# An attention kernel with a fused gated expert layer: another hand-written order for the first fourteen steps

## The chip, the cores and the metric

The kernel runs on one core of one Trainium2 chip. The metric is the device time of one execution in microseconds (us); smaller is better. The core has five engines with a queue each: PE (matrix products), DVE (vector work), ACT (functions of one input, scaled copies), POOL (vector work, slower, no access to the accumulators), and SP (which here only issues transfers). Each engine takes its instructions in the order of its own queue and waits on semaphores for the others.

## The reference

Two parts, all in float32, with inputs q, k, v of 4 batches, 8 heads, 768 positions, 64 features, and expert weights of 512 x 2048 and 2048 x 512:

```python
k_sum = k.reshape(B, H, nb, 32, D).max(axis=3)      # 24 block maxima of the keys
v_sum = v.reshape(B, H, nb, 32, D).mean(axis=3)     # 24 block means of the values
a = softmax(concat[mask_l(scale * q @ k.T), scale * q @ k_sum.T + log(32)])   # window of +-15
x = (a @ concat[v, v_sum]).reshape(3072, 512)
h = x @ w_in
P = a0 + a1*h + a2*h**2 + a3*h**3
Q = 1 + |b0|*|h| + |b1|*h**2
out = (P / (Q + 1e-6)) @ w_out
```

## The kernel before

**Tiling.** The 3072 rows go in six groups (g) of 512. The attention makes 64 rows at a time, a half, for all 8 heads; eight halves fill a group, halves 0 to 11 are batch 0 and 12 to 23 batch 1. The expert layer goes over 16 weight chunks (fc) of 128 columns. A step is one chunk of one group: 12 products of 128 x 512 for the first layer, a function of eight or nine vector passes, then 12 products for the second layer, which trails. A product in full precision is made of three: inputs and weights are split into a rounded part and a rest (xh and xl, gh and gl, and hi and lo of the weights).

**The order.** Steps 0 to 13 and all of the first sixteen halves are issued in the order of a list, `TEXT` (lines 48 to 59). Lines 721 to 723 turn each word into a call of `token` (line 670), and line 721 makes the order binding for all five queues: an instruction may not pass one that an earlier word put on the same engine. Between engines only data and buffers order the work. From step 14 on (line 734) a scheduler orders it. A word is a letter and a number; where a chain has several parts, each further occurrence issues its next part, written below as w9.2 for the second occurrence of w9:

- K, Q, V, A, W, I with a number: loads, all on SP. K: raw keys of batch 0 (four of 400 KB). Q: queries of the first group (two of 512 KB). V: the 96 value rows of a half (192 KB). A: queries and keys of a later half (two transfers, 128 and 192 KB). W: one weight chunk, both matrices (1024 KB). I: raw keys of batch 1 (384 KB). F and G: value rows for the block means of batch 0 (141 and 512 KB) and batch 1 (1024 and 512 KB). S: four small loads on ACT's queue (247 KB together) and three small DVE passes.
- k, i: block maxima of the keys, DVE. v, u: products that give the block means of batch 0 and 1, PE (ten and six). m: the means of batch 0 are copied into the value tiles of halves 0 and 1 by ACT and of halves 2 to 7 by POOL (line 214, `ENG_M`); no weighted sum of values may be issued ahead of it. n: the same for batch 1, with a store on SP.
- h: a half (line 324). For halves 0 to 7: h.1 scores on PE (a pair at once); h.2 four DVE passes; h.4 exponentials on ACT; h.5 reciprocal on DVE; h.6 the scaling, on DVE for halves 2 to 5 and else on POOL; h.7 four transposes on PE; h.8 their copy (DVE or ACT); h.9 the weighted sum on PE; h.10 xh (ACT or DVE); h.11 xl on DVE. From half 8 on one part comes first, the copy of the block maxima into the key tile (`key_blocks`, line 239: on DVE, or for half 12 a transfer on SP), so that all numbers are one higher.
- w: the split of a weight chunk (line 458): w.1 ACT, w.2 POOL, w.3 DVE, w.4 ACT (hi), w.5 DVE (lo). For chunks 5, 7 and 8 (`MODE`, letter e) w.5 is on ACT and w.6 a transfer issued by POOL.
- x: the first layer of a step in three parts, four products each (PE). y: the second layer in four parts of three products, the third of which reads gl. ga to gk: the function: a, b, d on ACT, c, e, f, i, j on DVE (i gives gh), k on POOL (gives gl).

**Buffers.** Some loads wait for buffers. W takes one of four tiles (line 453): W9 waits until w5 is done, W11 until w7 is done. Raw keys of batch 1 lie in `stage`, which has two buffers (line 90): the tiles of the last value rows of the first group, of G, and of the four I take them in turn. A load of I so waits for the readers of the tile two before it.

Of the kernel before, what the change touches and what calls it, by code (L numbers as in the profile page):

```python
# [822 lines left out]
```

## Time and profile before

| what | value |
|---|---|
| time of three runs, us | 637.99, 636.54, 637.9; median 637.9 |
| profiled execution: span from first to last instruction, us | 636.9 |
| median less span (what lies around the span), us | 1.0 |
| busy: PE, DVE, ACT, POOL, us | 620.4, 568.5, 457.1, 256.9 |
| first product of the expert layer, us from the span's start | 38.44 |
| last product of the list on PE (y10.4) ends, us | 136.3 |
| last DVE pass of the list (w15.3) ends, us | 141.8 |

Times in the trace are in us from the span's start. The trace gives one execution. A line of the timeline shows the start, the time, the engine, the operation with the tiles that it writes and reads, and in brackets the idle time before it and what ended that; neighbours of one kind are merged, and pipelined instructions overlap, so that the distance from one start to the next is what an instruction takes of its queue. All calls here go through one helper, so every row says L113; tiles tell them apart (wr raw weights; wearly and w split weights; ss, sm softmax; pt, pts transposed weights; av weighted sum; vf block means; kr raw keys of batch 1; h, po the two layers; gh, gl, ta, tq, tu the function). TensorE's granted clock is at full speed throughout the stretches used here.

### The profile page before, as it was taken

Reading aid. Unit: us, or ns where it says so; the run is one execution under the profiler, and the core shown is the slowest. Engines: PE = TensorE matmul, PEld = TensorE weight load, DVE = VectorE, ACT = ScalarE, POOL = GpSimd, SP = SyncE. Lnnn points to the kernel's source line nnn. Section 1 sums busy time; section 2 is a strip of 40 time slices with the busy share of each in tenths; the row PEclk is TensorE's granted clock in tenths of the full one; section 3 lists DMA queues with packets and bytes.
Section 4 is the critical chain, followed back from the end, with each engine's and each line's share of the span. In section 5 each row is a group of like instructions: output and inputs, shape, how many; then the busy total and the mean of one; then the engine's idle time right before and its main releaser. Section 6 shows DMA issues by size and latency. Waiting matters only on the chain.

```text
span 636.9 us, 11880 instructions
## 1 busy us (share of the span) xinstructions
PE 620.4 (97%) x4078; PEld 494.2 (78%) x4078; DVE 568.5 (89%) x1155; ACT 457.1 (72%) x1020; POOL 256.9 (40%) x344
## 2 busy tenths in 40 slices
PE   8899999999999999999999999999999999999997
PEld 4466777778788878888888777888888888888886
DVE  5799999999898999889988989988988989898885
ACT  3789999877867757767767768667777765656662
POOL 1366679654434336233143244243234242222221
PEclk9999999999999999999999999999999999999999
DMA  9977777413434434324423433323333120100001
GB/s 289 341 281 233 242 220 232 165 40 126 148 113 136 138 114 155 106 99 138 134 89 120 136 124 101 95 72 106 93 132 100 57 65 1 63 4 1 1 2 66
DMA packets 51752, 77.66 MB, mean 122 GB/s; under 512 B 6260, under 2 KB 33524, under 8 KB 49772
## 3 DMA queue, kind: packets, MB, share of 16 engines
q1 hardware_dynamic: 50412, 74.75, 36.2%
q0 software_dynamic: 560, 1.77, 1.4%
q8 instruction: 32, 0.52, 0.3%
q10 hardware_dynamic: 720, 0.38, 0.2%
q14 instruction: 28, 0.23, 0.1%
HBM read 60.33 MB, written 14.73 MB: 118 GB/s over the span
## 4 chain that ended last, share of the span: by engine, by line
PE 62%; DVE 21%; ACT 6%; DMA 5%; issue 3%; POOL 2%; DVEq 0%; POOLq 0%; ACTq 0%
PE po L113 29%; PE h L113 28%; DVE tu L113 6%; DVE tq L113 5%; PE av L113 3%; DVE gh L113 2%; PE sc L113 2%; DMA wr<-in_wio_dram 2%; DVE wr L113 2%; ACT ta L113 2%; DMA kres<-in_kraw_dram 1%; DVE ss L113 1%; POOL ss L113 1%; DMA w<-wr 1%; ACT ss L113 1%
## 5 line engine op out<-in xcount | busy, mean ns | idle before, releaser
L113 POOL TENSOR_TENSOR gl<-tu,ta 128x512 fp32r<-128x512 f32 x96 | 129.4, 1348 | 296.5 <-DVE tu L113 140.3
L113 ACT ACTIVATE ta<-tq,cs 128x512 f32<-128x512 f32 x96 | 69.8, 727 | 80.5 <-DVE tq L113 79.6
L113 PE MATMUL po<-wearly,gh 128*128 128x512 f32 x384 | 120.3, 394 | 0.7 <-ACT o L113 0.7
L113 PE MATMUL po<-w,gh 128*128 128x512 f32 x384 | 119.7, 393 | 0.0
L113 POOL TENSOR_SCALAR ss<-ss,sm 128x120 f32<-128x120 f32 x176 | 84.3, 497 | 41.6 <-DVE sm L113 40.7
L113 PE MATMUL h<-xh,wearly 128*128 128x512 f32 x384 | 97.8, 394 | 1.6 <-DVE tu L113 1.0
L113 PE MATMUL h<-xh,w 128*128 128x512 f32 x384 | 96.8, 391 | 1.4 <-DVE sm L113 0.9
L113 PEld LDWEIGHTS h<-xh,wearly 128*128 128x128 f32 x384 | 71.5, 188 | 18.2 <-ACT ta L113 1.0
L113 PEld LDWEIGHTS po<-wearly,gh 128*128 128x128 f32 x384 | 70.8, 188 | 18.0 <-ACT o L113 2.4
L113 PEld LDWEIGHTS h<-xh,w 128*128 128x128 f32 x384 | 71.5, 188 | 17.0 <-ACT ta L113 1.3
L113 DVE SCALAR_TENSOR_TENSOR gh<-tu,cs,ta 128x512 fp32r<-128x512 f32 x96 | 73.8, 768 | 10.9 <-ACT ta L113 1.4
L113 PEld LDWEIGHTS po<-w,gh 128*128 128x128 f32 x384 | 71.2, 188 | 15.7 <-issue 1.1
L113 ACT ACTIVATE ss<-ss,sm 128x120 f32<-128x120 f32 x188 | 71.7, 385 | 12.2 <-DVE sm L113 12.2
L113 ACT ACTIVATE tu<-h,cs 128x512 f32<-128x512 f32 x96 | 74.7, 778 | 0.5 <-PE h L113 0.5
L113 PE MATMUL po<-w,gl 128*128 128x512 f32 x192 | 74.9, 390 | 0.0
L113 PE MATMUL po<-wearly,gl 128*128 128x512 f32 x192 | 74.8, 390 | 0.0
L113 DVE SCALAR_TENSOR_TENSOR tu<-tu,cs,tq 128x512 f32<-128x512 f32 x96 | 72.2, 753 | 2.6
L113 DVE SCALAR_TENSOR_TENSOR tu<-tu,cs,h 128x512 f32<-128x512 f32 x96 | 71.1, 741 | 2.2
L113 DVE SCALAR_TENSOR_TENSOR tq<-tq,gh 128x512 f32<-128x512 f32 x96 | 66.6, 694 | 2.7
L113 ACT ACTIVATE ta<-h,cs 128x512 f32<-128x512 f32 x95 | 64.6, 680 | 4.8 <-POOL gl L113 4.8
L113 DVE TENSOR_TENSOR tu<-tu,h 128x512 f32<-128x512 f32 x96 | 64.9, 676 | 0.1
L113 ACT ACTIVATE ta<-ta 128x512 f32<-128x512 f32 x96 | 60.8, 633 | 2.7
(92 smaller groups left out, 917.3 us busy)
## 6 DMA issues: line engine op xcount, KB each, us to landing
wr<-in_wio_dram SPq DMA_DIRECT2D x15, 1024.0 KB
cross<-tb SPq DMA_DIRECT2D x32, 256.0 KB
vw<-in_vpad_dram SPq DMA_DIRECT2D x42, 192.0 KB
kw<-in_kwin_dram SPq DMA_DIRECT2D x40, 192.0 KB
pts<-cross SPq DMA_DIRECT2D x96, 64.0 KB
out_dram<-o SPq DMA_DIRECT2D x23, 256.0 KB
qw<-in_qw_dram SPq DMA_DIRECT2D x40, 128.0 KB
kr<-in_kraw_dram SPq DMA_DIRECT2D x12, 384.0 KB
```

Of the source, the lines that this page charges most:

```text
L113: out = getattr(self.engine, name)(*args, **kw)
```

## The change

Only `TEXT` differs. Both lists have the same 566 words, each the same number of times, so that every engine gets the same instructions, and the steps from 14 on are the same. What differs is the order on each queue. On SP the start goes from K2 K1 K0 Q0 K3 Q1 V2 V0 F0 V5 V1 W0 V6 V4 V3 V7 W1 A8 A9 W2 W3 G0 W4 to K1 K0 K2 K3 Q0 Q1 V2 F0 W0 W2 V5 V3 V4 V1 V7 V6 V0 A9 W1 W4 W3 W6 A8 G0. Chunks 0 and 2 are then split (w0 and w2) among the first softmax passes, ahead of m. Half 6 is the last of the first group on all its queues. Further on SP has ... I1 W5 A11 W7 n W8 I0 V8 I3 A12 I2 V9 A13 W9 W10 W11 h12.1 W15; POOL has ... gk2 gk3 w7.6 w9.2 h11.7 gk4 gk5; PE has ... x7.3 y3.4 y4.1 y5.1 y5.2 h12.2; DVE has ... gj4 i0 gc5 ge5 gf5 i2 gi5 h13.1 gj5 ge6 gc6 gf6 h8.12 w9.3 gc7 ge7 h10.6 h12.3.

```diff
--- before.py
+++ after.py
@@ -45,18 +45,18 @@
 LAG = 3
 SOFF = 12
 NWARM = 6
-TEXT = ("K2 K1 K0 Q0 K3 Q1 k2 k0 V2 V0 F0 V5 V1 k1 S0 k3 h0 h1 W0 V6 h0 V4 V3 h0 h1 h0 V7 W1 A8 h1 A9 h2 h3 h0 h2 h4 h3 v2 h1 h2 h3 h2 h4 v9 h0 h0 v0 h3 h1 h6 h2 v1 w0 h3 h2 W2 h3 "
-         "v5 h5 W3 h6 h5 h4 G0 h0 w0 h4 h4 w0 h4 v8 v6 v4 h5 h5 v3 h7 v7 h1 h1 m0 h5 h2 h0 h5 h7 h7 h3 h1 w0 h2 w0 h6 h0 h6 h0 h6 h4 h3 h2 h2 h1 h6 h1 h2 h7 h5 h3 h5 h3 h7 h1 h4 h7 "
-         "w1 h3 h5 h6 h5 h5 h6 h7 h4 W4 w1 h4 h7 w2 h7 h4 h6 w1 h7 h6 x0 w1 h7 h6 x0 x0 h8 w1 W5 h8 w2 u0 x1 w1 w2 w3 w3 ga0 I0 w3 gb0 x1 h8 ge0 h8 w2 gc0 w4 w1 x1 h9 gf0 u2 gd0 u1 "
-         "w2 w2 A11 h9 W6 gi0 I1 h9 w4 ga1 gj0 u3 h9 u4 A10 gb1 ge1 h8 w3 gc1 gf1 w3 gd1 V8 x2 gk0 h8 i0 x2 x2 gb2 ga2 gi1 ge2 h8 W7 u5 h9 w4 w5 gc2 h8 h9 w5 gj1 x3 V9 gf2 I2 w3 y0 "
-         "w4 gd2 i1 gk1 x3 x3 n0 h8 w4 w6 h10 x4 w5 h10 h8 h8 gi2 h8 gj2 ga3 h10 y0 gb3 h9 w5 y0 y0 h9 gk2 w5 h10 ge3 gc3 w6 gf3 V10 h11 h9 gd3 I3 A12 x4 i2 w5 x4 gi3 W8 h9 x5 h9 "
-         "y1 x5 y1 y1 h11 w6 gb4 gj3 A13 ga4 h10 V11 w6 ge4 h9 gf4 gc4 w6 w7 W9 h11 h11 x6 gk3 h10 gd4 y1 x5 gi4 x6 w8 w7 i3 h10 gj4 ga5 y2 y2 w7 gk4 h10 gb5 h12 h11 h10 x6 ge5 gc5 "
-         "h11 w8 y3 y2 gf5 h10 h10 w8 y3 y2 h10 W10 w6 y3 w7 w7 w7 x7 x7 gd5 ga6 gi5 y3 gj5 W11 V12 h11 gb6 w8 gk5 gc6 h12 ge6 h11 x7 x8 h13 w9 gf6 w8 y4 gd6 h11 w9 h13 h12 h11 w8 "
-         "V13 w9 h12 gi6 y5 y5 A14 x8 y5 gj6 ga7 y5 y4 gb7 y4 x8 gk6 h12 gc7 ge7 h13 w10 w10 h13 A15 h11 w9 h12 gf7 h11 y4 gd7 w9 gi7 h13 h14 W12 ga8 gb8 gj7 x9 w9 h12 w10 x9 gc8 "
-         "gk7 w10 y6 w11 h13 h12 ge8 gf8 w10 h12 x9 h12 h14 gd8 y6 w11 W13 x10 w11 y7 y6 y6 h12 gi8 h12 gj8 V14 h13 w12 w10 gb9 h13 ga9 A16 h15 x10 h14 ge9 gc9 h14 gk8 w11 h13 w11 "
-         "h15 w12 gd9 w13 h13 W14 x10 y7 W15 h13 gf9 gi9 w12 gj9 gb10 ga10 gc10 h14 ge10 y7 V15 x11 y7 h15 w12 x11 gk9 h15 w13 gd10 x11 gf10 h14 A17 x12 w12 gi10 w12 gj10 ga11 h15 "
-         "y8 h13 h14 gb11 w13 ge11 y8 x12 y8 y9 gc11 gf11 y8 h14 h15 x12 w13 y9 gd11 x13 w14 h14 w13 w14 y9 w14 h14 w13 gk10 w15 h14 y9 gi11 gb12 h14 h15 y10 gj11 ga12 gc12 ge12 "
-         "x13 w14 h15 gk11 w14 gf12 x13 w15 h15 w14 h15 gd12 h15 y10 gi12 y10 h15 gb13 ga13 ge13 gj12 gc13 y10 gf13 gd13 gk12 w15 w15 ")
+TEXT = ("K1 K0 K2 k1 K3 k0 k2 k3 Q0 h2 h3 h0 h1 S0 h2 h2 h2 h1 h0 h0 Q1 h4 V2 F0 v2 h6 h3 h10 h7 h0 h2 h2 h2 h1 h8 h9 h0 h0 h1 h1 h6 h1 h3 h3 h3 h0 h5 W0 h7 h0 v9 v8 h6 h6 h2 W2 h1 h3 "
+        "h3 V5 w0 w0 w0 v5 V3 h4 h6 h7 h7 h7 h1 v3 w2 w2 w2 V4 v4 h4 h5 h5 V1 v1 w0 w0 V7 v7 V6 v6 h4 h4 h4 V0 v0 A9 h4 w2 h15 h6 h6 h5 h3 h7 w2 h5 h5 h4 w2 m0 h1 h0 h1 h1 h0 h0 h7 h7 "
+        "h2 h2 W1 W4 w1 h2 w1 h4 h4 h4 h6 h5 h5 w1 h3 h3 h3 h7 h7 h7 W3 w3 w3 h5 h5 h5 h6 h6 h6 w3 w4 w4 w4 w1 W6 w1 w3 w3 x0 x0 x0 gb0 ga0 ge0 gc0 A8 h8 h9 h9 G0 h8 gf0 x1 x1 u0 x1 "
+        "w6 w4 A10 h9 u5 gd0 ga1 w6 w6 gi0 gj0 gc1 gb1 ge1 w4 u1 x2 x2 w3 h9 h9 gf1 x2 u4 ga2 gc2 h8 w1 I1 w1 W5 u3 gd1 gi1 A11 gk0 gb2 ge2 u2 W7 n0 gj1 w5 w5 w5 y0 h9 gf2 h8 h8 W8 "
+        "h11 h11 x3 x3 gd2 w5 gk1 x3 h11 I0 gi2 y0 i1 ga3 gc3 h8 w5 w5 x4 x4 gj2 h11 x4 V8 gb3 h10 w8 ge3 h10 gf3 y0 y0 y1 y1 y1 y1 x5 x5 h9 w7 w7 w7 h11 h11 I3 i3 gd3 gi3 h8 w8 w8 "
+        "ga4 x5 gc4 w7 gj3 gb4 A12 I2 gk2 y2 y2 y2 ge4 gf4 w6 x6 w6 y2 gk3 y3 gd4 gi4 h10 w7 w7 y3 h8 x6 x6 y3 V9 gj4 i0 ga5 gc5 gb5 ge5 gf5 h10 x7 i2 w8 h8 gd5 gi5 A13 w6 h9 x7 h13 "
+        "gj5 gb6 ga6 ge6 w8 gc6 gf6 h8 h8 W9 W10 w9 w9 w9 h11 gk4 x7 ga7 gc7 h14 W11 gb7 ge7 gk5 h10 y3 y4 y5 y5 h12 h12 h12 h13 gf7 gd6 w10 w10 w10 gd7 y5 W15 gi6 gi7 h11 h11 y5 y4 "
+        "gj6 w8 w9 x8 w9 w9 w10 w15 A14 h13 h13 h12 h9 V11 h9 h9 A15 w10 w10 x8 x8 w11 w11 w11 x9 ga8 gc8 y4 y4 gb8 ge8 W12 w15 V10 h12 gk6 y6 y6 gj7 h11 h12 w11 gd8 h14 h14 h14 w12 "
+        "w11 y6 y6 x9 x9 gb9 ga9 gf8 h10 h10 h10 x10 x10 h11 gi8 gj8 h13 ge9 x10 W13 gc9 gd9 h11 gf9 h14 w15 gi9 h13 w12 h15 h15 h15 gk7 y7 h14 gj9 h10 V12 h12 y7 y7 V13 h10 w12 y7 "
+        "ga10 gk8 h15 x11 x11 y8 y8 x11 gb10 ge10 w13 w13 gc10 h15 w12 h12 h12 h13 y8 gf10 x12 h10 gd10 h13 y8 W14 ga11 h13 w12 w12 w13 w13 gk9 gi10 gc11 gj10 gb11 x12 h12 h12 h13 V15 "
+        "h13 h13 h14 gk10 w13 y9 w14 w14 A17 w13 x12 ge11 h12 gf11 h14 h14 V14 y9 y9 gd11 y9 y10 y10 gi11 ga12 gc12 gb12 ge12 x13 gj11 h15 h14 w14 gf12 A16 h14 h14 gd12 x13 gi12 gk11 "
+        "w14 w14 gj12 gk12 y10 y10 h15 h15 x13 ga13 gc13 gb13 ge13 h15 h15 h15 gd13 gf13 w14 w15 ")
 AVGW = NK + NB - 4
 AVGH = NK + NB - 2
 NREST = (S - HPG * HQ) // P
```

## Rows read from the trace of the kernel before

**Rows 1.** The windows view over four stretches, of which three rows: from start to end in us, length, then busy time of PE, weight loads, DVE, ACT and POOL (each with its instructions), granted clock, share of the transfer engines, GB/s.

```profile
0.00:38.44 38.44, 32.84 (x448) 19.52 (x448) 25.77 (x104) 22.10 (x78) 15.18 (x31) 1.00 0.99 327
38.44:136.30 97.86, 94.15 (x603) 70.96 (x604) 96.43 (x191) 91.99 (x185) 68.85 (x62) 1.00 0.63 202
136.30:200.00 63.70, 62.61 (x409) 50.74 (x408) 58.22 (x131) 48.43 (x117) 25.77 (x42) 1.00 0.37 118
```

**Rows 2.** The timelines of PE and DVE around the end of the list: y10.4, its last product; w15.3, its last DVE pass; a later wait of PE.

```profile
135.61 0.61 PE L113 MATMUL po<-w,gh 128*128 128x512 f32 x2
...
163.97 1.15 PE L113 MATMUL av<-pts,vw 120*64 120x64 f32 x32 [0.55 <-DVE tu L113]
...
140.47 1.37 DVE L113 SCALAR_TENSOR_TENSOR wr<-wr 128x512 int32<-128x512 int32 x2
```

**Rows 3.** The chain of waits (start, duration, what): the first chunk of weights, from issue to landing.

```profile
10.06 12.52 DMA wr<-in_wio_dram
```

**Rows 4.** The timelines of DVE and ACT: the wait of a reciprocal for the exponentials behind that chunk; the copies of the block means (m).

```profile
25.50 0.18 DVE L113 RECIPROCAL sm<-sm 128x4 f32<-128x4 f32 x1 [3.53 <-ACT sm L113]
...
27.25 1.06 ACT L113 COPY vw<-vf 24x512 f32<-24x512 f32 x2
```

**Rows 5.** The timeline of SP: issues of K3, W0, V6, and of the second transfers of A8 and of A9.

```profile
4.60 0.34 SPq L113 DMA_DIRECT2D kres<-in_kraw_dram  x1
...
10.06 0.35 SPq L113 DMA_DIRECT2D wr<-in_wio_dram  x1
12.00 0.31 SPq L113 DMA_DIRECT2D vlast<-in_vpad_dram  x1
...
17.11 0.33 SPq L113 DMA_DIRECT2D kw<-in_kwin_dram  x1
...
23.23 0.33 SPq L113 DMA_DIRECT2D kw<-in_kwin_dram  x1
```

**Rows 6.** The timeline of PE: the block means from V6, then from V4 and V3; the first product of the expert layer.

```profile
23.26 1.12 PE L113 MATMUL vf<-vlast,kres 96*120 96x512 f32 x2 [0.83 <-DMA vlast<-in_vpad_dram]
24.22 1.95 PE L113 MATMUL vf<-vr,kres 96*120 96x512 f32 x4
...
38.44 2.11 PE L113 MATMUL h<-xh,wearly 128*128 128x512 f32 x8 [0.47 <-ACT xh L113]
```

**Rows 7.** The timeline of POOL: the scaling of a half early and late, the copies of the block means to halves 2 to 5 and to 6 and 7, w.2 of a chunk, gl of a step.

```profile
14.18 1.39 POOL L113 TENSOR_SCALAR ss<-ss,sm 128x120 f32<-128x120 f32 x4
...
27.97 2.35 POOL L113 COPY vr<-vw 24x512 f32<-24x512 f32 x4 [2.73 <-ACT vw L113]
30.26 2.17 POOL L113 COPY vlast<-vw 24x512 f32<-24x512 f32 x2
...
60.46 4.90 POOL L113 TENSOR_SCALAR ss<-ss,sm 128x120 f32<-128x120 f32 x4
...
95.73 1.13 POOL L113 TENSOR_SCALAR wr<-wr 128x1024 int32<-128x1024 uint8 x1
...
132.75 1.29 POOL L113 TENSOR_TENSOR gl<-tu,ta 128x512 fp32r<-128x512 f32 x1 [0.81 <-DVE tu L113]
```

**Rows 8.** The groups by line and shape over the first 235 us: busy time, mean ns of one. DVE: w.3; xl; the copy of block maxima; c; e; f; i; the second pass of j; a block maximum of raw keys. POOL: one of the four passes that scale a half.

```profile
L113 POOL TENSOR_SCALAR ss<-ss,sm 128x120 f32<-128x120 f32 x80 | 45.2, 583 | 8.5 <-DVE sm L113 7.7
...
L113 DVE SCALAR_TENSOR_TENSOR gh<-tu,cs,ta 128x512 fp32r<-128x512 f32 x29 | 23.5, 810 | 2.4 <-PE po L113 0.5 <-ACT ta L113 0.2
...
L113 DVE SCALAR_TENSOR_TENSOR tu<-tu,cs,tq 128x512 f32<-128x512 f32 x29 | 21.7, 750 | 0.7
L113 DVE SCALAR_TENSOR_TENSOR tu<-tu,cs,h 128x512 f32<-128x512 f32 x29 | 21.4, 737 | 0.3
...
L113 DVE TENSOR_TENSOR tu<-tu,h 128x512 f32<-128x512 f32 x29 | 19.6, 678 | 0.1
L113 DVE SCALAR_TENSOR_TENSOR wr<-wr 128x1024 int32<-128x1024 int32 x15 | 18.7, 1250 | 0.3 <-issue 0.2
...
L113 DVE SCALAR_TENSOR_TENSOR tq<-sq,cs,ta 128x512 f32<-128x512 f32 x19 | 14.2, 746 | 1.8 <-ACT ta L113 1.7
...
L113 DVE TENSOR_REDUCE ks<-kr 128x24 f32<-128x768 f32 x8 | 7.5, 936 | 0.0
...
L113 DVE TENSOR_TENSOR xl<-av,xh 128x256 fp32r<-128x256 f32 x16 | 6.6, 414 | 0.5 <-ACT xh L113 0.5
...
L113 DVE COPY kw<-ks 128x96 f32<-128x96 f32 x5 | 1.3, 289 | 0.0
```

**Rows 9.** The timelines of PE and SP: the last block mean of batch 1 (it ends at 53.30), and the issue of I1.

```profile
52.28 1.02 PE L113 MATMUL vf<-vf,kres 128*120 128x512 f32 x2
...
53.33 0.33 SPq L113 DMA_DIRECT2D kr<-in_kraw_dram  x1
```

**Rows 10.** The view of the transfers by line: those of half a chunk that POOL issues (KB each, median us from issue to landing).

```profile
wearly<-wr POOLq DMA_DIRECT2D x2, 512.0 KB, 5.3
...
w<-wr POOLq DMA_DIRECT2D x1, 512.0 KB, 8.7
```

**Rows 11.** The chain of waits (start, duration, what): all three parts of a first layer and all four of a second layer on PE; and, from the timeline of PE, the scores of two halves.

```profile
169.07 2.72 PE h L113 x12
171.79 2.72 PE po L113 x12
...
41.40 1.05 PE L113 MATMUL sc<-kw,qw 64*64 64x120 f32 x32
```

## Prediction

> **What bounds the kernel now.** I read the windows view first, then the timelines of the engines around its edges, then the chain of waits. Up to the first product of the expert layer at 38.44 the transfer engines are 0.99 busy, and DVE works 25.8 of 38.4 us. From there to the last product of the list DVE is busy for 96.4 of 97.9 us and PE for 94.2. Behind the list DVE falls to 58.2 of 63.7 us and PE stays at 62.6 [rows 1]. So the kernel has three stages: loads decide until 38, DVE until about 142, PE for the rest. PE's list ends at 136.3, DVE's only at 141.8, and even then PE waits for DVE once more, 0.55 us at 163.97 [rows 2]. A delay of DVE within the list therefore reaches the end nearly in full, and so does a gain, for behind the list nothing that is saved can be lost again: PE works there almost without gaps.
>
> In the first stage the chain of waits goes through the first chunk of weights: issued at 10.06, landed 12.52 us later [rows 3]. ACT stands for it, and a reciprocal on DVE, behind exponentials that wait on ACT, stands 3.53 us [rows 4]. That hole is what there is to win at the start. The new list holds the same instructions, so I ask two things only: how much DVE work is done when the expert layer begins, and whether DVE then finds its operands in time.
>
> **The start.** The loads go out in order. Up to W0, SP and ACT have issued 5.3 MB before, 4.7 MB in the new list (four value rows of 192 KB later, one of them ahead of F as before); up to W2 it is 5.8 MB, up to V5 6.0, up to V0 7.1. To put clocks on these I take the landings of before: W0 at 22.6 [rows 3]; the second transfer of A8 goes out at 17.11, when V1, eight loads ahead of it (4.3 MB in the order), can have landed; K3 goes at 4.60 in the same way; the second of A9 at 23.23, with V6 landed [rows 5, 6]. That is 5.5 us for the megabyte around W0. On the same curve W0 lands at 19.5 to 20.5 in the new list, W2 at about 24.4 and V5 at 25.0.
>
> Here the list pays. The value rows now land behind W2, and the seven block-mean products that need them stand in a row on PE, about 0.9 us each (two of them 1.95) [rows 6]: 25.0 + 7 x 0.9 = 31.3 for m, against 27.25 [rows 4]. From m on, POOL copies the means to halves 2 to 7; before this began 0.7 behind m and took 2.35 + 2.17 us [rows 7], now until 36.5. Only then comes w1.2, 1.1 us [rows 7], and w1.3 on DVE, 1.2 us [rows 8], ahead of the last five passes of the first group: 36.5 + 1.1 + 1.2 + three of the five at 0.35 = 39.9 for the first product of step 0, against 38.44 [rows 6]: 1.5 us later. At that point DVE has done w2.3 and w2.5 (2 x 1.2) and two copies of block maxima (2 x 0.29) [rows 8] that before came later: 3.0 us. Net the start gives DVE 3.0 - 1.5 = 1.5 us. If W2 lands 1.5 us sooner it is 3.0; if 2 us later it is -0.5. PE's own work ahead of step 0 is the same in both lists.
>
> **The middle.** Most words have slack, by counting the work ahead of them on their queues. One place has not. The raw keys of batch 1 lie in two buffers, and I2 takes that of I0. In before this kind of wait shows: I1 goes out at 53.33, as the product that reads the buffer's last tenant ends at 53.30 [rows 9]. The new list has i1 i3 i0 i2 on DVE, with i0 late, behind j4. So I2 goes out behind i0, and with it all that SP holds behind I2: V9, the two transfers of A13, W9, W10, W11, and the key tile of half 12 (h12.1). On POOL, w9.2 stands ahead of the scaling of half 11, gk4 and gk5. On PE, y4.1 needs gk4, y5.1 needs gk5, and h12.2 stands behind both; on DVE, h12.3 needs h12.2. From the end of i0 to h12.3:
> - four issues ahead of W9 at 0.35 or more [rows 5], with gaps 1.8;
> - W9 from issue to landing: no row shows one alone. Half a chunk from POOL takes 5.3 and 8.7 [rows 10], the first, behind 4.3 MB, 12.5 [rows 3]; 4.3 would be 2 MB (all from I2 to W9) at the 0.327 MB per us of the start [rows 1], 6.1, less the 1.8 above. I take 5.3, between 4.3 and 8.7;
> - w9.2 1.1; the scaling 4 x 0.58 = 2.3 (1.4 to 4.9); gk4 1.3 [rows 7, 8];
> - gk5 1.3, then the third product of y5.1 0.2, y5.2 0.7, the scores 1.05 [rows 11]: 3.3.
>
> The sum is 1.8 + 5.3 + 1.1 + 2.3 + 1.3 + 3.3 = 15.1, with ends 12.8 (1.4 + 4.3 + 1.1 + 1.4 + 1.3 + 3.3) and 21. Meanwhile DVE has from i0 to h12.3: c, e, f of step 5, i2, i5, a copy, j5 (two), e, c, f of step 6, an xl, w9.3, c and e of step 7, a reciprocal. By the means that is 0.75 + 0.68 + 0.74 + 0.94 + 0.81 + 0.29 + 1.5 + 0.68 + 0.75 + 0.74 + 0.41 + 1.25 + 0.75 + 0.68 + 0.17 = 11.1 [rows 4, 8]; neighbouring passes overlap a little, so 10.4. **DVE stands for 15.1 - 10.4 = 4.7 us**, between 2.4 and 10.6. PE stands as well: gk4 comes 11.8 after i0, while PE needs 2 for f5 and then x7, half 8's sum, y3.4 and two thirds of y4.1, 4.5: 5.3 us. The wait of i2 for I2 itself lies inside.
>
> A second path confirms the place: h12.1 is a transfer of 48 KB issued behind three chunks. In before the 192 KB of V6, issued 1.9 us behind W0, are awaited by PE until 23.26, just after W0's 22.58 [rows 3, 5, 6]: a small load behind a large one lands after it. The Trainium skill says so too ("DMA: Bandwidth & Descriptors", section Queues, rings and completion order: each engine consumes its ring in order), and by that three megabytes stand ahead of the scores; the sum doesn't use it.
>
> The same page of the Trainium skill gives in Anatomy of one DMA a fit, 2.0 us plus the bytes by 436 GB/s, for transfers that POOL issues; W9 would take 4.4 us, an estimate by that page, and DVE's stand would be 3.8. For half a chunk it gives 3.2 where the rows have 5.3 and 8.7, so the rows are taken.
>
> Elsewhere two small waits of PE may come (x4.1 behind f2, x8.3 behind the rest of chunk 8 that POOL issues late, 8.7 to land [rows 10]); DVE doesn't wait for them, and I put them at 0, at 2 if DVE is nearer than I count.
>
> **The sum.** DVE ends its list 4.7 - 1.5 = 3.2 us later. PE is late by 1.5 + 5.3, less what it waits for DVE anyway in the list, 97.9 - 94.2 = 3.7 [rows 1]: 3.1. Both say about 3, and behind the list some tenths come back. Span 636.9 + 3.1 = 640.0; with the 1.0 between the span and the median of the three runs, **641.0 us**.
>
> **Rivals.**
> 1. The wait is at its low end (2.4) and the start gains 3.0: 636.9 + 2.4 - 3.0 + 1.0 = 637.3, no change. For it: in the stretches of SP where W9 comes, the transfer engines are 0.63 busy or less [rows 1]; against: I2, V9 and A13 go out just ahead of it.
> 2. Faster. The buffer that I2 takes may be free earlier than I read, so that I2 and W9 go out some 15 us sooner. This decides: hanging on i0, W9 would have to land within 0.6 us (10.4 less the other 9.8) to cost nothing, and not hanging on it costs nothing. Then the start's 1.5 to 3.0 stay: 634.9 to 636.4, taken as 635.4. For it: DVE is full in this stage and the work moved ahead of step 0 is real. Against: SP's waits in before fit two buffers taken in turn [rows 9].
> 3. Slower still. W2 lands 2 us or more later than the curve, as W0 did with 5.5 us for its megabyte, m moves with it, and W9 takes 8.7: -0.5 and 8: 646.
>
> **How the numbers follow.** Forecast 0.50, rival 1 0.22, rival 2 0.17, rival 3 0.11. A measurement of this kernel tells about 0.3%, 1.9 us, from no change, that is 636.0 and 639.8. The forecast's own ends (639 to 643.5) lie for the most part above that: slower 0.60, same 0.23, faster 0.17. For the range I leave out half of rival 2 and a part of rival 3: 635.8 to 645.5.
>
> **What would show it.** Right: the first product of step 0 at 39 to 41; I2 issued within 0.2 us of i0's end; on POOL one idle time ended by a raw chunk's landing at about 85, then PE idle 4 to 6 us ahead of a product that reads gl, and DVE 3 to 7 us ahead of the softmax passes of half 12, near 90 to 95. Wrong: no hole on DVE between 80 and 100, or the first product at 37 or before.

## The result and the profile after

The new list takes 643.73 us (median of 4 runs, 641.74 to 644.86) where the kernel before takes 637.22 on the same chip (4 runs, 636.54 to 637.99): **ratio 1.0094, 95% interval 1.0072 to 1.0117**, slower by 0.9%. Forecast were 641.0, with 0.60 on slower. The profiled execution took 643.42 with a span of 641.6, 4.7 more than the trace of before; that one is among the longer executions of its kernel (eight others, on another chip, had spans of 635.0 to 635.7), which is why the traces lie closer together than the medians. In every run with both on record the time is 1.8 us above the span.

The windows view, as in [rows 1], with the edges moved to the new first product and to the end of PE's new list (the weighted sum of half 15); two of its rows:

```profile
0.00:40.01 40.01, 31.14 (x448) 19.03 (x448) 29.51 (x110) 24.36 (x81) 20.47 (x32) 1.00 0.93 314
40.01:141.46 101.45, 95.56 (x603) 72.00 (x603) 97.00 (x187) 89.34 (x181) 57.01 (x61) 0.98 0.63 193
```

In the long middle stretch DVE is busy for 97.0 of 101.5 us, where [rows 1] had 96.4 of 97.9: a hole of more than 3 us has come in. Its list ends at 145.54 instead of 141.84.

**The start** came at the times forecast. The timelines of POOL (w2.2, a pass on the second weight chunk), ACT (the block means m), POOL (their copies to halves 2 to 5) and PE (step 0), the answers to [rows 4, 6, 7]:

```profile
21.57 1.10 POOL L113 TENSOR_SCALAR wr<-wr 128x1024 int32<-128x1024 uint8 x1 [1.05 <-DMA wr<-in_wio_dram]
...
30.57 1.06 ACT L113 COPY vw<-vf 24x512 f32<-24x512 f32 x2
...
31.75 2.64 POOL L113 COPY vr<-vw 24x512 f32<-24x512 f32 x4
...
40.01 3.39 PE L113 MATMUL h<-xh,wearly 128*128 128x512 f32 x8 [0.47 <-DVE xl L113]
```

m is there at 30.57 (27.25 before; forecast 31.3), the first product at 40.01 (38.44; forecast 39.9). W2 landed at 21.5, not at 24.4. Not forecast: its eight products take 3.39 us instead of the 2.11 that they took before. The windows around them say why; the column after POOL is the granted clock:

```profile
38.00:40.00 2.00, 1.15 (x32) 1.01 (x32) 1.51 (x6) 0.56 (x3) 1.92 (x2) 1.00 0.97 361
40.00:42.00 2.00, 1.99 (x6) 1.55 (x7) 2.00 (x4) 2.00 (x3) 0.20 (x1) 0.62 1.05 396
42.00:44.00 2.00, 2.00 (x7) 1.57 (x5) 2.00 (x3) 1.16 (x2) 0.00 (x0) 0.52 0.59 214
44.00:60.00 16.00, 16.00 (x98) 10.61 (x97) 14.35 (x34) 14.84 (x33) 8.53 (x9) 1.00 0.64 209
```

At 0.5 PE runs at 1.2 instead of 2.4 GHz. It had been busy for 1.15 us of the 2 before, and 6.91 of the 10 before. From 44 on it has no gap for 16 us, while DVE is busy for 14.35; in the kernel before it was the other way round (h12_copy below has the same start without the fall):

```profile
44.00:60.00 16.00, 14.84 (x54) 9.47 (x53) 15.66 (x33) 15.82 (x36) 8.16 (x9) 1.00 0.75 268
```

**The middle** did not. The timelines of DVE (i3; i0), of SP (I2; W9, W10 and W11 as one line; the key tile of half 12), of POOL (the third stage of chunk 7; w9.2), of PE (the last product group of step 7; the scores of half 12) and of DVE (the softmax of half 12):

```profile
70.21 0.92 DVE L113 TENSOR_REDUCE ks<-kr 128x24 f32<-128x768 f32 x1
...
79.72 0.95 DVE L113 TENSOR_REDUCE ks<-kr 128x24 f32<-128x768 f32 x1
...
71.15 0.33 SPq L113 DMA_DIRECT2D kr<-in_kraw_dram  x1
...
73.01 13.75 SPq L113 DMA_DIRECT2D wr<-in_wio_dram  x3
...
86.86 0.53 SPq L113 DMA_DIRECT2D kw<-ks  x1
...
77.52 0.90 POOL L113 DMA_DIRECT2D wearly<-wr  x1 [0.97 <-ACT pts L113]
...
80.07 1.11 POOL L113 TENSOR_SCALAR wr<-wr 128x1024 int32<-128x1024 uint8 x1 [1.66 <-DMA wr<-in_wio_dram]
...
86.42 1.19 PE L113 MATMUL h<-xh,wearly 128*128 128x512 f32 x4 [0.73 <-DMA wearly<-wr]
...
91.85 1.86 PE L113 MATMUL sc<-kw,qw 64*64 64x120 f32 x32 [1.49 <-DMA kw<-ks]
...
92.92 0.28 DVE L113 CUSTOM_DVE_ANT_0 ss<-sc,mask 128x120 f32<-128x120 f32 x1 [1.84 <-PE sc L113]
```

I2 goes out at 71.15, right behind i3 (which ends at 71.13), not behind i0 (which ends at 80.67). So W9 goes out at 73.0 and lands 7.1 us later (taken: 5.3), w9.2 starts at 80.07, and no product stands for gl. But the line of three issues lasts until 86.76: W11 takes the raw tile of chunk 7, which a transfer of POOL reads from 77.5 to 86.4. The key tile of half 12 is queued behind it, PE stands 1.49 us for that tile, and DVE 1.84 for the scores: the second path of the prediction.

**Longer passes.** DVE's total work in the list is the same, yet its busy time up to the list's end is 130.54 us instead of 127.71. The difference sits in a few passes. The timelines of DVE and POOL, three pairs (the first with POOL's scaling passes just ahead):

```profile
112.83 1.84 DVE L113 SCALAR_TENSOR_TENSOR tq<-tq,cs,ta 128x512 f32<-128x512 f32 x1
...
110.97 1.92 POOL L113 TENSOR_SCALAR ss<-ss,sm 128x120 f32<-128x120 f32 x3
112.86 1.26 POOL L113 TENSOR_TENSOR gl<-tu,ta 128x512 fp32r<-128x512 f32 x1
...
129.99 2.30 DVE L113 TENSOR_TENSOR w<-wr,w 128x1024 fp32r<-128x1024 f32 x1
...
129.92 1.29 POOL L113 TENSOR_TENSOR gl<-tu,ta 128x512 fp32r<-128x512 f32 x1 [5.72 <-DVE tu L113]
...
59.34 1.22 DVE L113 SCALAR_TENSOR_TENSOR wr<-wr 128x1024 int32<-128x1024 int32 x1
...
59.57 2.14 POOL L113 TENSOR_TENSOR gl<-tu,ta 128x512 fp32r<-128x512 f32 x1 [0.71 <-DVE tu L113]
```

The c pass of step 9 (0.75 elsewhere in the list) begins at 112.83, while POOL is in its last scaling pass (to 112.89), with gl right behind; gl ends at 114.12, and DVE's pass 0.55 later. The low part of a chunk (1.22 elsewhere) begins 0.07 behind gl and ends 1.08 behind gl's end. In the third pair DVE began first, keeps its 1.22, and POOL's pass (1.29 elsewhere) lasts 2.14. Behind step 0 five DVE passes are held in this way by 0.7 us or more in the new list (at 68.20, 100.92, 112.83, 120.11 and 129.99: 4.8 us together beyond their own length), two in the kernel before (74.09 and 110.86: 1.85 us). The Trainium skill has it as a rule ("SBUF — State Buffer", section SBUF: two separate sides): GpSimd (POOL here) shares a pair of SBUF ports with DVE, and whichever begins first, a GpSimd pass or a DVE pass that has two SBUF inputs or runs in a mode with two ports, keeps the pair to its end. These rows agree with it: the five held passes have both operands in SBUF.

**Behind the list** weighted sums on PE, which follow the one at 163.97 of [rows 2], before (the fourth) and after (the first and the fourth):

```profile
237.43 1.15 PE L113 MATMUL av<-pts,vw 120*64 120x64 f32 x32 [1.21 <-DVE tu L113]
```

```profile
167.89 1.15 PE L113 MATMUL av<-pts,vw 120*64 120x64 f32 x32
...
242.51 1.15 PE L113 MATMUL av<-pts,vw 120*64 120x64 f32 x32 [1.51 <-DVE tu L113]
```

The delay is 3.9 us at the first, where PE waited 0.55 before and does not now, and 5.1 at the fourth. Over the whole rest about 1 us more is lost where I expected some tenths back. The windows from the end of DVE's list to the end of the span, before and after:

```profile
141.84:636.91 495.07, 488.34 (x2982) 399.84 (x2980) 440.82 (x853) 340.72 (x755) 171.42 (x249) 1.00 0.29 92
145.54:641.60 496.06, 489.30 (x3000) 400.94 (x2990) 440.64 (x853) 340.72 (x755) 172.14 (x249) 1.00 0.29 91
```

PE stands as long as before (6.76 us for 6.73) but has 0.96 us more to do: when DVE's list ends, PE has got less far.

### The profile page after: what moved, and what is told of

Read it like the earlier page. It is cut to its first block, busy times and chain, and to the rows that moved or that the text cites. A ratio compares the mean times of both kernels' runs of the same rounds, so it can differ in the third digit from the quotient of the medians.

```text
span 641.6 us, 11880 instructions
## 1 busy us (share of the span) xinstructions
PE 619.9 (97%) x4078; PEld 494.9 (77%) x4078; DVE 571.2 (89%) x1155; ACT 457.2 (71%) x1020; POOL 251.0 (39%) x344
## 4 chain that ended last, share of the span: by engine, by line
PE 48%; DVE 29%; ACT 7%; issue 6%; DMA 5%; POOL 4%; DVEq 0%; SPq 0%; ACTq 0%; POOLq 0%
PE po L113 23%; PE h L113 22%; DVE tu L113 10%; DVE tq L113 8%; DVE gh L113 4%; DMA wr<-in_wio_dram 3%; POOL ss L113 2%; ACT ss L113 2%; ACT ta L113 2%; DVE ss L113 2%; PE av L113 1%; PE sc L113 1%; DVE wr L113 1%; DVE w L113 1%; DVE ks L113 1%
## 5 line engine op out<-in xcount | busy, mean ns | idle before, releaser
L113 POOL TENSOR_TENSOR gl<-tu,ta 128x512 fp32r<-128x512 f32 x96 | 131.2, 1366 | 298.8 <-DVE tu L113 141.2
L113 ACT ACTIVATE ta<-tq,cs 128x512 f32<-128x512 f32 x96 | 69.6, 725 | 79.7 <-DVE tq L113 78.6
L113 PE MATMUL po<-wearly,gh 128*128 128x512 f32 x384 | 121.1, 396 | 0.6 <-ACT o L113 0.6
L113 PE MATMUL po<-w,gh 128*128 128x512 f32 x384 | 119.8, 393 | 0.0
L113 PE MATMUL h<-xh,wearly 128*128 128x512 f32 x384 | 99.0, 397 | 2.1 <-DVE tu L113 0.9
L113 PE MATMUL h<-xh,w 128*128 128x512 f32 x384 | 96.6, 391 | 1.8 <-DVE tu L113 1.7
L113 POOL TENSOR_SCALAR ss<-ss,sm 128x120 f32<-128x120 f32 x176 | 78.2, 463 | 43.9 <-DVE sm L113 43.3
L113 PEld LDWEIGHTS h<-xh,wearly 128*128 128x128 f32 x384 | 72.3, 190 | 19.6 <-DMA wearly<-wr 1.2
L113 PEld LDWEIGHTS h<-xh,w 128*128 128x128 f32 x384 | 71.7, 188 | 17.6 <-ACT pts L113 1.7
L113 PEld LDWEIGHTS po<-wearly,gh 128*128 128x128 f32 x384 | 70.6, 188 | 18.7 <-ACT o L113 2.5
L113 DVE SCALAR_TENSOR_TENSOR gh<-tu,cs,ta 128x512 fp32r<-128x512 f32 x96 | 75.1, 783 | 11.0 <-ACT ta L113 2.0
L113 PEld LDWEIGHTS po<-w,gh 128*128 128x128 f32 x384 | 71.1, 188 | 15.6 <-issue 1.1
L113 ACT ACTIVATE ss<-ss,sm 128x120 f32<-128x120 f32 x188 | 71.7, 384 | 14.0 <-DVE sm L113 13.8
L113 ACT ACTIVATE tu<-h,cs 128x512 f32<-128x512 f32 x96 | 74.6, 777 | 3.7 <-POOL gl L113 2.2
L113 PE MATMUL po<-wearly,gl 128*128 128x512 f32 x192 | 74.9, 390 | 0.0
L113 PE MATMUL po<-w,gl 128*128 128x512 f32 x192 | 74.8, 390 | 0.0
L113 DVE SCALAR_TENSOR_TENSOR tu<-tu,cs,tq 128x512 f32<-128x512 f32 x96 | 72.2, 752 | 2.6
L113 DVE SCALAR_TENSOR_TENSOR tu<-tu,cs,h 128x512 f32<-128x512 f32 x96 | 71.1, 741 | 2.2
L113 DVE SCALAR_TENSOR_TENSOR tq<-tq,gh 128x512 f32<-128x512 f32 x96 | 66.3, 690 | 2.6
L113 ACT ACTIVATE ta<-h,cs 128x512 f32<-128x512 f32 x95 | 64.5, 678 | 3.9 <-POOL gl L113 3.9
L113 DVE TENSOR_TENSOR tu<-tu,h 128x512 f32<-128x512 f32 x96 | 64.9, 676 | 1.0 <-ACT ta L113 1.0
L113 ACT ACTIVATE ta<-ta 128x512 f32<-128x512 f32 x96 | 60.7, 632 | 2.7
```

The source lines that it names most:

```text
L113: out = getattr(self.engine, name)(*args, **kw)
```

## The experiments

Twelve kernels ran. The table has the ratio to the kernel before, then from one profiled execution the first product of step 0, the end of DVE's list, the idle time of DVE ahead of and behind the first product (gaps of its timeline, summed), its busy time up to the list's end, and the span, all in us. Rows of the experiments say L111 or L113, as their list takes fewer lines or not.

| kernel | ratio (95%) | first product | list end | idle ahead | idle behind | busy | span |
|---|---|---|---|---|---|---|---|
| before | 1 | 38.44 | 141.84 | 12.70 | 1.43 | 127.71 | 636.9 |
| the new list | 1.0094 (1.0072 to 1.0117) | 40.01 | 145.54 | 10.51 | 4.49 | 130.54 | 641.6 |
| h12_copy | 1.0074 (1.0049 to 1.0100) | 39.64 | 143.08 | 10.07 | 2.80 | 130.21 | 639.5 |
| port_moves | 1.0053 (1.0036 to 1.0070) | 40.45 | 142.86 | 10.68 | 3.12 | 129.06 | 639.1 |
| copy_and_moves | 1.0068 (1.0045 to 1.0091) | 40.08 | 144.41 | 10.77 | 5.20 | 128.44 | 640.9 |
| pe_filled | 1.0094 (1.0079 to 1.0109) | 39.91 | 145.76 | 10.99 | 4.28 | 130.49 | 642.2 |
| keys_in_turn | 1.0193 (1.0177 to 1.0208) | 38.72 | 150.68 | 9.73 | 11.30 | 129.65 | 646.8 |
| c9_from_psum | 1.0164 (1.0144 to 1.0183) | 39.38 | 148.25 | 10.36 | 8.00 | 129.89 | 644.6 |
| chunk7_early | 1.0059 (1.0040 to 1.0077) | 40.01 | 144.99 | 10.25 | 3.16 | 131.58 | 641.2 |
| new_start_old_rest | 1.0031 (1.0017 to 1.0044) | 40.59 | 142.98 | 10.77 | 4.07 | 128.14 | 638.0 |
| early_first_old | 1.0012 (1.0003 to 1.0021) | 38.65 | 142.05 | 10.09 | 4.07 | 127.89 | 636.7 |
| early_first_new | 1.0083 (1.0064 to 1.0102) | 41.16 | 146.96 | 13.23 | 3.81 | 129.92 | 643.1 |
| old_start_new_rest | 1.0124 (1.0106 to 1.0142) | 38.86 | 148.32 | 13.09 | 4.31 | 130.92 | 644.8 |
| before_moves | 0.9990 (0.9977 to 1.0003) | 37.43 | 139.87 | 11.25 | 1.35 | 127.27 | 634.7 |

Loads land up to 3 us apart from one execution to the next (the first product of the same start lies between 38.7 and 40.6), so single traces are compared by their own stretches.

**keys_in_turn**: the buffer as the prediction read it.

```diff
- ... gb4 A12 I2 gk2 ... y3 V9 gj4 i0 ga5 ...
+ ... gb4 A12 gk2 ... y3 gj4 i0 I2 V9 ga5 ...
-    sums = {}
+    sums, keep = {}, {}
...
-            kr = stage.tile([P, S], F32, tag="st", name=f"kr{bi}_{pr}")
+            if pr == 2:
+                kr = keep[0]
+            else:
+                kr = keep[pr] = stage.tile([P, S], F32, tag="st", name=f"kr{bi}_{pr}")
```

> The new list with the buffer as I had read it: the raw keys I2 go into the buffer of I0, so that I2 and V9 are issued behind the reduction i0 (near 80.6 instead of 71.1), and all that SP holds behind them too. The forecast's chain (W9 lands 9 us later, then w9.2, the scaling of half 11, gk4, gk5 on POOL, then the scores of half 12): DVE stands 4.7 us more than without that wait, W9 lands near 88, gk4 comes near 93, and the time is 3 to 5 us above the new list, ratio 1.014 to 1.017. Rival: W11 waits until 86.4 for the rest of chunk 7 in any case, and the holes are shared: at most 1.5 us above, ratio 1.009 to 1.012.

The timelines of SP (I2), POOL (w9.2), ACT (b of step 6), PE (the product that reads gl of step 4) and DVE (e of step 6):

```profile
77.84 0.33 SPq L111 DMA_DIRECT2D kr<-in_kraw_dram  x1
...
86.68 1.08 POOL L111 TENSOR_SCALAR wr<-wr 128x1024 int32<-128x1024 uint8 x1 [11.13 <-DMA wr<-in_wio_dram]
...
90.50 0.78 ACT L111 ACTIVATE tu<-h,cs 128x512 f32<-128x512 f32 x1 [9.63 <-POOL gl L111]
...
90.52 0.79 PE L111 MATMUL po<-wearly,gl 128*128 128x512 f32 x1 [5.64 <-POOL gl L111]
...
92.47 0.69 DVE L111 TENSOR_TENSOR tu<-tu,h 128x512 f32<-128x512 f32 x1 [8.24 <-ACT ta L111]
```

1.0193: about 6 us above the new list, more than the forecast's chain gave and above the ratio expected here. The chain is there as written. W9 lands 6.9 us behind its issue at 79.8 (taken: 5.3, between 4.3 and 8.7), and PE stands 5.64 us for gl (forecast 5.3). DVE stands 8.24 instead of 4.7: the work that I counted against the wait was itself behind gk4. tu has two buffers, so b of step 6 waits 9.63 us for POOL, and e, c and f of step 6 and all behind them wait for b. It is within the bounds given (2.4 to 10.6), by a reason that was not.

**h12_copy**: the second path alone.

```diff
-KDMA = "00111000"
+KDMA = "00110000"
```

> The new list, but the block maxima of half 12 are copied into its key tile by DVE (one pass of about 0.2 us) instead of by a transfer that goes out behind three chunks of weights. Theory 1 (this transfer is what DVE stands for, 1.84 us ahead of the softmax of half 12): the scores no longer wait, DVE's hole near 92 closes, and the end comes 1.0 to 1.8 us sooner, ratio to the kernel before about 1.007. Theory 2 (the new list is slow because DVE passes with two operands in SBUF start just behind a POOL pass and wait for it, five times about 1 us; the hole is filled by nothing that matters): within 0.5 us of the new list, ratio 1.009. Theory 3 (the late and slow first step decides, everything behind it is only shifted): no change, 1.009 to 1.010.

1.0074. In the trace DVE's hole ahead of half 12 is 1.18 us instead of 1.84, so the transfer is worth 0.7 there, and behind it stand the chunk's landing (step 7 still waits 0.96 us) and a pass of ACT (0.44 us ahead of the scores). The list ends 2.5 us sooner than in the trace of the new list, but 1.9 of that are there at 62 already: this execution had no fall of the clock in step 0. So theory 1 is right in kind, and small; the interval overlaps that of the new list, so that the time alone shows no gain. The windows from 0 to 62 us of the kernel before, of the new list and of this run:

```profile
0.00:62.00 62.00, 55.24 (x575) 34.42 (x577) 48.96 (x150) 44.43 (x121) 27.46 (x41) 1.00 0.86 290
...
0.00:62.00 62.00, 53.12 (x564) 34.41 (x565) 49.84 (x156) 44.29 (x121) 31.18 (x42) 0.97 0.85 288
...
0.00:62.00 62.00, 52.74 (x573) 34.61 (x574) 51.34 (x159) 46.18 (x124) 32.87 (x45) 1.00 0.87 299
```

Where the clock doesn't fall, DVE has been busy for 2.4 us more than before by then; in the new list's trace for 0.9 more.

**port_moves**: four DVE passes moved.

```diff
- ... w7 w7 w7 h11 h11 I3 i3 gd3 ... gj8 h13 ge9 x10 W13 gc9 gd9 ...
+ ... w7 w7 h11 h11 I3 i3 w7 gd3 ... gj8 h13 gc9 ge9 x10 W13 gd9 ...
- ... V13 h10 w12 y7 ... V15 h13 h13 h14 gk10 w13 y9 ...
+ ... V13 w12 h10 y7 ... V15 h13 w13 h13 h14 gk10 y9 ...
```

> The new list with four DVE passes moved by one to three places, no work changed: the shift of chunk 12 and the low part of chunk 13 directly behind the product that releases POOL's gl pass, the c pass of step 9 ahead of e of step 9, the shift of chunk 7 behind the last key reduction but two. Theory 2 (a DVE pass with two SBUF operands that starts after a POOL pass waits for POOL's end, and the other way round POOL waits): the four passes, now 1.84 to 2.33 us, fall to 0.75 and 1.22, POOL's passes beside them rise to about 2.1; DVE's list ends 2.5 to 4 us sooner, ratio 1.003 to 1.006. Theories 1 and 3 (the transfer of half 12, the first step): the passes are long for another reason (a transfer or a late operand that the profile counts into them) and stay long wherever they stand, ratio 1.009.

1.0053: the list ends at 142.86 and the time falls by 0.4% with no work taken away. This execution had no fall of the clock either. The shift of chunk 12 and the low part of chunk 13 on DVE, and the gl pass beside the latter on POOL:

```profile
118.68 1.22 DVE L111 SCALAR_TENSOR_TENSOR wr<-wr 128x1024 int32<-128x1024 int32 x1
...
127.95 1.22 DVE L111 TENSOR_TENSOR w<-wr,w 128x1024 fp32r<-128x1024 f32 x1
...
128.21 2.10 POOL L111 TENSOR_TENSOR gl<-tu,ta 128x512 fp32r<-128x512 f32 x1 [5.09 <-DVE tu L111]
```

1.22 where the new list has 2.33 and 2.30; now POOL waits (2.10). All four moved passes are at 0.88 or 1.22. Others are held instead (four by more than 0.7 us between 22 and 109, at places where the new list has none), which is why 1.5 us of busy time are won, not 4. Theory 2 stands.

**copy_and_moves**: both edits.

> The new list with both edits: the block maxima of half 12 copied by DVE, and the four DVE passes moved. Alone they measured 1.0074 and 1.0053 where the new list has 1.0094. If the hole ahead of half 12 and the passes that wait for POOL are two separate losses, the gains add: 1.0020 to 1.0040. If they are one loss (the moved passes already let the transfer of half 12 come in time), 1.0048 to 1.0060, as with the moves alone.

1.0068, its interval overlapping that of the moves alone: the gains do not add. The hole that the copy closes was closed already in port_moves (no wait there ahead of half 12); with both it is 1.18 us again. This execution had the fall of the clock (the first eight products took 3.66 us). The two do not add, then; that the one limit stands close behind the other is argued, and which one the combined kernel meets is not shown.

**c9_from_psum**: one operand of one held pass in PSUM.

```diff
-SQ_PS = "011001101001110"
+SQ_PS = "011001101101110"
```

> The new list, with the squares of step 9 in PSUM instead of SBUF, so that the c pass of step 9 reads one operand from each. It took 1.84 us, begun 0.03 us before a POOL pass of 1.26 us. Theory 2 with two SBUF operands as the condition: 0.75 us, beside a POOL pass that runs at the same time; the time falls by 0.5 to 1.1 us, ratio 1.0075 to 1.0085. If any DVE pass beside POOL's can be held: it stays above 1.4 us, ratio 1.009.

The pass itself (DVE), the gl pass beside it (POOL), and a wait of PE just behind:

```profile
111.85 0.75 DVE L111 SCALAR_TENSOR_TENSOR tq<-sq,cs,ta 128x512 f32<-128x512 f32 x1
...
111.87 1.26 POOL L111 TENSOR_TENSOR gl<-tu,ta 128x512 fp32r<-128x512 f32 x1
...
112.74 0.62 PE L111 MATMUL pt<-ident,ss 128*120 128x128 f32 x4 [4.18 <-DVE tq L111]
```

It begins 0.02 us ahead of POOL's pass, both run at once, and it takes 0.75 us. The other traces say the same on a larger scale: of all c passes in the 14 traces, 785 have their squares in PSUM, 653 of them overlap a pass of POOL, and none takes more than 0.75 us; 545 have both operands in SBUF, and 359 of them take 1.0 to 1.9 us. Each of the 359 begins while POOL is in a pass or, 33 of them, at most 0.05 us ahead of one, and ends 0.54 to 0.55 us behind that pass; within such a distance the rows don't tell which came first. Two inputs are not always needed: in this trace a copy from SBUF to SBUF of 0.20 us, the block maxima of a half, took 1.29 at 81.93, beside a gl pass. The whole kernel is slower, 1.0164, for a side effect: the squares now take one of the two PSUM tiles that the transposed weights of a half need, and PE stands 4.18 us for it. What the clock does then is in the section on the hardware.

**pe_filled**: PE kept busy ahead of step 0.

```diff
- ... h3 h3 h3 h7 h7 h7 W3 ... w1 w3 w3 x0 x0 x0 ...
+ ... h3 h3 h3 h7 f4 h7 h7 W3 ... w1 w3 w3 f1 x0 x0 x0 ...
+        elif kind == "f":   # n products of ident by mask into a spare tile
...
```

> The new list with five products of identity by mask (about 0.4 us each, into a spare PSUM tile) on PE in the two holes ahead of step 0, four at 36.7 and one at 39.5. Theory 3 (PE's clock fell to half in step 0 because PE stood so much in the 10 us before): the granted clock stays 1.0 from 40 to 44, the first eight products take 2.1 us instead of 3.4, step 0's h is there 1.3 to 1.6 us sooner, DVE's hole of 1.00 at 46 closes, and the end comes 0.8 to 1.6 us sooner, ratio 1.007 to 1.008. Theory 4 (the clock falls for another reason, or DVE doesn't need h sooner): first products still 3.4 us, or the time as it is, 1.009.

PE is busy for 9.05 us of the 10 ahead of step 0, the clock stays at 1.0 there, the first products take 2.17 us, the hole of 1.00 is gone, and the time is the same, 1.0094. DVE is 1.6 us ahead at 62, 0.6 at 92 and not at all at the list's end: the transfer of chunk 7 lands at 85.9 all the same (PE stands 1.82 us for it), and DVE waits 1.45 and 1.00 us. As the only cause theory 3 falls.

**new_start_old_rest** and **old_start_new_rest**: the two parts of the change alone, spliced behind x0; what one start had done and the other had not is left out or put in right there.

> The order of the new list up to the products of step 0, and behind it the order of before, less what is done already. DVE stands 2.2 us less ahead of step 0 in the new list (10.5 us for 12.7). If the start is a gain that the rest of the new list loses: ratio 0.9965 to 0.999. If the gain is lost right behind the start in any order (first product 1.6 us later, DVE then waits for step 0 and for POOL's part of the weights): 0.9995 to 1.004.

> The order of before up to the products of step 0, then what the new list had done by then (chunks 2, 3 and 4), then the rest of the new list. If the rest is what costs: ratio 1.008 to 1.013. If the start is what costs: 1.000 to 1.004.

1.0031 and 1.0124. The rest of the new list costs 6.5 us at the list's end (148.32 for 141.84): 2.9 in waits, 3.2 in longer passes, 0.4 ahead. Of the waits 1.25 us stand right behind the splice, where three chunks are made up for, so that the 6.5 is an upper bound. The new start isn't a gain even with the old rest. The timelines of PE (first product) and DVE (e of step 2), and the windows view from 44 to 60:

```profile
40.59 2.11 PE L111 MATMUL h<-xh,wearly 128*128 128x512 f32 x8 [0.47 <-DVE xl L111]
...
56.64 0.69 DVE L111 TENSOR_TENSOR tu<-tu,h 128x512 f32<-128x512 f32 x1 [2.04 <-ACT ta L111]
```

```profile
44.00:60.00 16.00, 15.91 (x81) 10.56 (x73) 13.11 (x35) 13.35 (x33) 5.79 (x7) 1.00 0.61 202
```

Ahead of step 0 DVE stands 1.93 us less than before, and behind it 2.64 more. PE is busy for 15.91 of the 16 us: what DVE has done ahead, it waits for.

**early_first_old** and **early_first_new**: the shift of chunk 1 behind the last passes of the first group.

```diff
- ... h6 h5 h5 w1 h3 h3 h3 h7 ... h6 h6 h6 w3 w4 ...
+ ... h6 h5 h5 h3 h3 h3 h7 ... h6 h6 h6 w1 w3 w4 ...
```

> The new start with the old rest, and one pass moved: the shift of chunk 1 on DVE (1.2 us and the 1.0 us that it waits for POOL) stands behind the last five passes of the first group instead of ahead of them; step 0 needs chunk 0 alone. With the new start and the old rest the first product came at 40.6 and the ratio was 1.0031. If the start's gain is lost because step 0 begins 2 us late and DVE then waits for step 0 and its followers: first product at 38.2 to 38.8, DVE's holes of 2.04 and 0.42 behind it shrink by 1.5 in sum, ratio 1.0000 to 1.0015. If the holes come from POOL's late part of the weights or from the loads: first product earlier but the same time, 1.0025 to 1.0035.

> The new list whole, with the same one pass moved. Start theory: the first product near 38.3 instead of 40.0, the holes of 1.00 and 0.55 behind step 0 close, and 1.0 to 1.5 us are won: ratio 1.007 to 1.008. If what is won there is lost again where the third stage of chunk 7 lands and W11 waits for it (near 86, as with the filled PE): 1.009 to 1.010.

With the old rest 1.0012 for 1.0031, in the range that was expected of an earlier first product; the two intervals just overlap. From m to the first product it took 8.2 and 7.9 us in these two traces, 8.7 to 10.4 in the nine others with this start. The timelines of PE and DVE:

```profile
38.65 2.11 PE L111 MATMUL h<-xh,wearly 128*128 128x512 f32 x8 [0.47 <-DVE xl L111]
...
43.77 1.12 PE L111 MATMUL vf<-vf,kres 128*120 128x512 f32 x2 [1.12 <-DMA vf<-in_vpad_dram]
...
55.86 0.69 DVE L111 TENSOR_TENSOR tu<-tu,h 128x512 f32<-128x512 f32 x1 [2.07 <-ACT ta L111]
```

The hole has not shrunk (2.07), as I had expected it to; it comes 0.8 us sooner. The first product came 1.9 us sooner, and PE lost 1.1 of that to a late load of G; from there on it has no gap, and DVE waits for ACT and ACT for PE. So in this stretch DVE goes at PE's pace. With the new rest 1.0083, whose interval overlaps the new list's; its loads were late in the profiled execution (41.16). It decides nothing.

**chunk7_early**: the third stage of chunk 7 sooner.

```diff
- ... gc4 w7 gj3 gb4 A12 I2 gk2 y2 ... h10 w7 w7 y3 ...
+ ... gc4 w7 w7 gj3 gb4 A12 I2 gk2 w7 y2 ... h10 y3 ...
```

> The new list with the last two steps of chunk 7 moved: ACT's negation directly behind its copy (at 73 instead of 75.9) and POOL's transfer that adds the whole directly behind gk2 (issued near 74.2 instead of 77.5). Theory 5 (this transfer, 8.9 us from issue to landing, is what the middle waits for: the last product of step 7 stands for it at 86.4, and W11, which takes the raw buffer that it reads, goes out at 86.4 and with it the key tile of half 12): it lands near 83, W11 goes out near 83, the key tile at 84, DVE's hole of 1.84 us ahead of half 12 falls below 0.7 and the wait of 0.73 at step 7 is gone; 1.0 to 2.0 us sooner, ratio 1.0065 to 1.0080. Rival (the transfer only takes longer, since W9 and W10 are under way at the same time, and lands at 85 or later; or PE stands for ACT's results instead): 1.009.

The timelines of SP (W9 to W11) and POOL (the transfer):

```profile
73.57 12.46 SPq L111 DMA_DIRECT2D wr<-in_wio_dram  x3
...
74.98 0.90 POOL L111 DMA_DIRECT2D wearly<-wr  x1 [3.07 <-DVE tq L111]
```

Issued at 74.98, 2.5 us sooner, it still holds W11 until 86.03: 11 us instead of 8.9, beside the same megabytes. No wait of DVE over 0.25 us is left between 65 and 145, but two more passes are held (1.88 and 1.73 us), and the trace is only 0.4 us shorter. The ratio, 1.0059, is better than the trace explains: the profiled execution is the longest of six (642.97; median 641.97). What made the others shorter stays open.

**before_moves**: the two held passes of the kernel before.

```diff
- ... gf4 gc4 w6 w7 W9 h11 h11 x6 ... gk8 w11 h13 w11 h15 ... h13 gf9 gi9 ...
+ ... gf4 gc4 w7 W9 h11 w6 h11 x6 ... gk8 w11 h13 gf9 w11 h15 ... h13 gi9 ...
```

> The kernel before with two passes moved, no work changed: the low part of chunk 6 behind the softmax passes of half 11, and the f pass of step 9 ahead of the low part of chunk 11. In the kernel before these two passes of the low part take 2.15 and 2.14 us, behind a POOL pass on the weights that began in the SBUF-only c pass just ahead. Theory 2: they fall to 1.2 to 1.6 us, 1.0 to 1.5 us in sum, and DVE's list ends as much sooner: ratio 0.9975 to 0.9990. If a shorter pass there is only a longer wait elsewhere: 0.9995 to 1.0010.

The two passes take 1.34 and 1.50 us instead of 2.15 and 2.14; one that was not held before now is (2.17 us for 1.22, at 54.42). 0.9990, with 1 inside the interval: perhaps the fastest of all kernels here, not shown to be faster than before.

## Why the prediction came out as it did

The sign was right and the time (641.0 for 643.73) near, but the change is twice the forecast: 6.5 us between the medians for 3.1. And it was luck in large part: neither of the two terms of the sum came as written, a gain of 1.5 us at the start and a wait of 4.7 for gl, and most of what the list lost was not in it. Of the signs of being right, the first product came; the issue of I2, the landing near 85, the wait for gl and the size of DVE's hole did not.

- **The start, its clock times: right, with help.** m, the copies and the first product came within 1.0 us. But W2 landed 2.9 us sooner than the curve (21.5 for 24.4), and by the prediction m would have moved with it. It did not: the products of the block means began at 23.8, behind transposes on PE that stood 1.28 us for ACT.
- **The start, its worth: wrong.** The step "net the start gives DVE 3.0 - 1.5 = 1.5 us" rests on "a delay of DVE within the list reaches the end nearly in full, and so does a gain". DVE stood even 2.2 us less ahead of step 0. With the old rest that is lost within 20 us, since PE is the bound there (15.91 of 16 us): the start alone costs 0.3%, and 0.1% with the shift of chunk 1 moved. With the new rest it depends on the clock. The new list's trace had lost most of the gain by 62; h12_copy and pe_filled, without the fall, still had it at 62, and pe_filled lost it behind that, at the waits and held passes of the middle.
- **The place in the middle: the step that failed is "I2 goes out behind i0".** It goes out behind i3, 9.5 us ahead of i0's end. I counted the tiles of the buffer in turn; what decides is which of the two is free at that place of the list, and there i3 stands ahead of I2 and i0 behind it. That much is rival 2's mechanism, but rival 2 held that nothing costs then, and that was wrong too. Where I2 does wait for i0 (keys_in_turn), the chain costs what was forecast and more; its mis-sized terms are W9's landing (6.9 us for 5.3) and DVE's cover of 10.4 us, about half of which, from e of step 6 on, needed gk4. The other price that the prediction names for W9, 4.4 us, is one for transfers that POOL issues; SP issues W9, and it took 6.9 and 7.1.
- **The second path: right in kind, left out of the sum.** The key tile behind three chunks makes the hole at 92.92, in the range of places that I had named (DVE near 90 to 95), of 1.84 us instead of 3 to 7. Two things hold it, the third stage of chunk 7 and the queue behind W11.
- **Not seen: DVE passes that wait for POOL.** The neighbouring rows of 2.15 us were in the trace of before; I took means. 2.8 us of the 3.7 at the list's end, by the account below. How much of the time they cost is shown in part: moving four of them gave 0.4%.
- **Not seen: 1 us behind the list.** The prediction had "behind the list some tenths come back". All kernels with the new rest lose 1.0 to 1.4 us there (span less list end, against before), those with the old rest lose nothing (0.0 to 0.4 less). It is work that PE still has to do at that point and not longer waits (488.34 and 489.30 us busy, 6.73 and 6.76 idle), so DVE's list end was not the right mark for PE. Why PE is behind is not shown.
- **A term of the sum was taken wrongly.** The 1.0 us between span and median is 1.8 in every run; it was the span of a long execution set against the median of others.

In the traces the list's end moves by -2.19 (less idle ahead) + 3.06 (more idle behind) + 2.83 (longer passes) = 3.70, and 1.0 comes behind. That is an account of two traces. No run brings the new rest below 1.0053, so what is left when the held passes and the hole are mended stays open.

## What to carry to other kernels

Work that one engine does ahead of a stage is worth something only if that engine is still the bound in the stages that follow: compare the busy shares of the next stretches, and the time of the stage's first product, before booking it. In an order written by hand, a DVE pass with both operands in SBUF goes directly behind the DVE pass that releases POOL's; a short pass in between let POOL start first here, and DVE's pass then ended about 1 us behind POOL's. The other order makes POOL wait, and other passes may be held instead: here four were. Which of two buffers a load takes is read from the list at its place, or from the issue times, not by counting in turn.
